# Even and odd value columns as the two halves, and an earlier order of loads, in a fused attention and MLP kernel

## The chip, the cores and the metric

The kernel runs on one core of one Trainium2 chip. The time is the device time of one execution in microseconds (us). For each kernel I quote the median of the fast runs and their range. A run more than 1.5% above the fastest of its kernel counts as slow and is left out. The kernel before took 374.89 us (three runs, 374.56 to 375.86).

The engines are named as the profile names them: PE is the matmul engine (TensorE), PEld its weight loads, DVE the vector engine, ACT the scalar engine, POOL the GpSimd engine, SP the sync engine. A "q" behind a name (SPq, POOLq) means that the engine issued a DMA.

## The reference, cut to what matters

Causal attention with a decay, over 8 batches, 8 heads, 576 tokens and 64 columns a head; then a dense two-layer MLP on the 4608 tokens, whose 512 input channels are the 8 heads side by side.

```python
cum = np.cumsum(np.log(np.clip(f, 0.0001, 1.0)), axis=-1)
scores = q @ k.T / 8 + cum[:, :, :, None] - cum[:, :, None, :]      # causal
attn = softmax(scores)
x = (attn @ v).transpose(0, 2, 1, 3).reshape(B * S, H * D)         # channel = 64 * head + column
h = x @ w_in                                                       # 512 -> 2048
out = (h / (1 + np.exp(-h))) @ w_out                               # 2048 -> 512
```

Everything is fp32 outside; the kernel works in bf16. The decay on the key's side is one weight per key, so the kernel multiplies the value rows by it.

## The kernel before

The work on TensorE is one long list. The first 128 tokens of each batch ("first blocks") are done first, since they give the MLP something to do: `turn0` transposes q and k, `scores0` makes scores and exponentials, `convert_v0` turns the fp32 value rows into weighted bf16 ones on GpSimd, `out0` multiplies and divides, `back0` transposes the result into the MLP's input. The remaining tokens follow in a main loop (`scores`, `attend`, `divide`). MLP chunks fill TensorE's gaps: `fill(us)` takes steps until that many microseconds are spent.

```python
def load_v0(b):
    t = stage.tile([P, H, D], FP32, ...)
    nc.sync.dma_start(out=t[:, :, :], in_=v[b, :, 0:P, :].rearrange("h p d -> p h d"))

# one chunk cc = (g, e) of 128 channels: half e (columns 32e to 32e+31) of the four heads j of group g
w_in_v = moe_w_in.rearrange("(g j e r) f -> g e j r f", g=NCC // 2, j=4, e=2)
def load_w_in(c0, c1):
    for cc in range(NCC):                                     # NCC = 4 chunks
        nc.gpsimd.dma_start(out=w_in_bf[:, cc, c0:c1], in_=w_in_v[cc // 2, cc % 2, :, :, c0:c1])

def after(ap):                    # the sync queue waits here until that piece of a weight has landed
    nc.sync.dma_start(out=junk[0:1, 0:16], in_=ap)

def convert_v(b, c):                                          # 32 of them; convert_v0, 8, is alike
    nc.gpsimd.tensor_tensor(
        out=vp[r, c, :, :],
        in0=vst[b][c][r, :, :],
        in1=w_bf[r, c + 1, b * H : (b + 1) * H, None].to_broadcast([n, H, D]),
        op=ALU.mult,
    )
# ... cut ...
def step():                       # one MLP chunk: up-projection m1 (x -> h), or down-projection m2 (h -> out)
    if can1 and can2:
        can1 = f1 <= f2 or g1 > g2 + 1        # alternate, by the share done of each
    ...

weights_scan()
turn0(0); turn0(1); weights(); scores0(0); convert_v0(0)
turn0(2); convert_v0(1); load_w_in(0, W1)                     # W1 = half of the 2048 columns
out0(0); scores0(1); turn0(3); convert_v0(2); back0(0)
out0(1); scores0(2); convert_v0(3); back0(1)
out0(2); scores0(3); back0(2); out0(3); back0(3)
ready.add(0)
# ... cut: the second half of w_in in two quarters, with q and k of batches 4 and 5 between ...
fill(7.0)
convert_v0(4); convert_v0(5)
for i in range(WQ): load_w_out(i)
after(w_out_bf[0:1, NFC - 1, DM - 16 : DM])
# ... cut: loads of the main loop's first q, k and of batch 0's value rows ...
two_more(4, 0.9)                                              # first blocks of batches 4 and 5
while at["m1"] < NFC: step()
ready.add(1)
while at["m1"] < 2 * NFC: step()
open2["w"] = True
fill(8.0)
convert_v0(6); convert_v0(7)
two_more(6, 0.9)
cast_qk(0); cast_qk(1); transposes(0); transposes(1)
for c in range(NM): convert_v(0, c)
while at["m2"] < M2_OF[0]: step()
ready.add(2)
# ... cut: the main loop ...
```

The softmax here doesn't subtract the row's maximum and nothing guards it: scores larger than these inputs give would overflow.

## Time and profile before

| Reading (kernel before) | us |
|---|---|
| median time; span of the profiled execution | 374.9; 373.9 |
| PE busy | 343.8 (92%) |
| first MLP matmul; MLP matmuls without a stall from | 26.3; 28.5 |
| first half of w_in landed; all of w_out landed | 28.5; 58.4 |
| first transposes for the main loop issued; first main scores | 75.2; 79.7 |
| one value conversion on GpSimd | 1.08 to 1.11 |

The whole page first: busy time of each engine with the number of instructions; TensorE's busy share and its granted clock in tenths over 40 equal slices of the span (9.3 us each); the queue of GpSimd's DMAs with packets, megabytes and share; two groups of instructions (what comes out, what goes in, count, total busy us, mean ns, idle before).

```profile
PE 343.8 (92%) x3621; PEld 190.4 (51%) x3621; DVE 206.5 (55%) x334; ACT 237.4 (64%) x416; POOL 148.0 (40%) x248
...
PE   2759999969997998899799999999999999999994
...
PEclk9957999969999999999999999999999999999998
...
q0 software_dynamic: 10752, 6.31, 11.6%
...
L358 POOL TENSOR_TENSOR vp<-vf,w_bf 128x512 bf16<-128x512 f32 (+1 forms) x32 | 34.3, 1079 | 6.8 <-DMA vf<-in_v_dram 6.1
...
L291 POOL TENSOR_TENSOR v<-vf,w_bf 128x512 bf16<-128x512 f32 x8 | 8.9, 1107 | 14.8 <-DMA vf<-in_v_dram 9.6
```

TensorE is the bottleneck, and the digits show where it isn't full: in the first three slices, in the ninth (75 to 84 us), and here and there up to the twentieth. The rest is solid. The clock digits fall in the third and fourth slices and in the ninth.

The waits of TensorE (total us, times, longest) show the two that belong to the MLP: for `gt`, the activation of an up-projection, and for `osb`, an output buffer.

```profile
PE hp L482 <- DVE gt L491: 8.3, 10, 1.4
...
PE hp L482 <- ACT osb L517: 2.8, 1, 2.8
```

By stretches (window; its length; PE, PEld, DVE, ACT and POOL busy with instructions; granted clock; DMA share; GB/s), nearly all of the 8.3 us lies before 212 us, and TensorE is full after it:

```profile
92.00:212.00 120.00, 111.56 (x1333) 59.66 (x1333) 74.91 (x105) 86.74 (x146) 58.52 (x95) 1.00 0.68 147
212.00:340.00 128.00, 128.00 (x1341) 70.24 (x1339) 76.81 (x121) 90.31 (x162) 46.95 (x74) 1.00 0.48 106
```

What the ninth slice waits for is on the sync queue's timeline (start us, length us, what). The line `junk<-w_out_bf` is the wait for w_out; everything behind it stands in a line.

```profile
58.37 0.50 SPq L188 DMA_DIRECT2D junk<-w_out_bf  x1
...
73.54 1.58 SPq L520 DMA_DIRECT2D out_dram<-osb  x3
75.23 2.98 SPq L372 DMA_TRANSPOSE qkT<-qkb  x2
```

TensorE's timeline gives the other ends: one turn of q and k (32 matmuls), the first long run of MLP matmuls, and the first scores of the main loop. The bracket is the idle time before it and what ended it.

```profile
14.79 1.08 PE L251 MATMUL tp<-sel,qkb 128*64 128x64 bf16 x32
...
28.51 9.70 PE L482 MATMUL hp<-x,w_in_bf 128*128 128x512 bf16 x33 [0.23 <-DMA w_in_bf<-in_moe_w_in_dram]
...
79.68 0.61 PE L402 MATMUL sc<-qkT 64*128 64x128 bf16 x8 [0.37 <-DMA qkT<-qkb]
```

So two chains run beside TensorE's work. One goes from the first blocks to the MLP's start. The other goes from w_out through the sync queue to the transposes and the main loop's start.

### The profile page before, as it was taken

To read this page: it belongs to the slowest core of one execution; us is meant where nothing else is said; L and a number is where in the kernel's file an instruction comes from. 1 tells how busy PE (TensorE), PEld (TensorE's weight loads), DVE (VectorE), ACT (ScalarE), POOL (GpSimd) and SP (SyncE) were. 2 spreads that over 40 slices of the span, in tenths; PEclk is the share of its full clock that TensorE was granted. 3 is DMA by queue.
4 is the path that set the end of the run, shared out by engine and by line. 5 is a ranking of instruction groups with operands and counts; after the bars stand their busy time and mean duration, and the time that the engine had idled before them with its cause. 6 is when DMAs were issued, how large, how long until landed. Compare 5 with 4: busy or idle time off the path is not lost.

```text
span 373.9 us, 9022 instructions
## 1 busy us (share of the span) xinstructions
PE 343.8 (92%) x3621; PEld 190.4 (51%) x3621; DVE 206.5 (55%) x334; ACT 237.4 (64%) x416; POOL 148.0 (40%) x248
## 2 busy tenths in 40 slices
PE   2759999969997998899799999999999999999994
PEld 2623575536644444455454555655554555555652
DVE  3644881425557656663754956656756656443430
ACT  4534782448875857767777878679779675445331
POOL 6656711360963740922734464464464301000000
PEclk9957999969999999999999999999999999999998
DMA  8599796899569538756954985984963000100112
GB/s 159 93 135 182 121 205 128 193 244 188 128 158 216 120 97 186 171 93 143 199 125 98 198 132 139 223 171 99 198 134 79 30 30 29 57 30 30 56 57 56
DMA packets 143066, 47.95 MB, mean 128 GB/s; under 512 B 132720, under 2 KB 137840, under 8 KB 143024
## 3 DMA queue, kind: packets, MB, share of 16 engines
q1 hardware_dynamic: 132272, 41.06, 49.9%
q0 software_dynamic: 10752, 6.31, 11.6%
q8 instruction: 28, 0.46, 0.5%
q14 instruction: 14, 0.11, 0.1%
HBM read 36.85 MB, written 9.44 MB: 124 GB/s over the span
## 4 chain that ended last, share of the span: by engine, by line
PE 67%; DMA 14%; DVE 6%; ACT 4%; SPq 3%; issue 3%; POOL 2%; ACTq 0%; POOLq 0%
PE po L508 29%; PE hp L482 23%; PE dn L433 8%; PE sc L402 6%; DMA w_out_bf<-in_moe_w_out_dram 4%; DMA vf<-in_v_dram 4%; DVE rec L456 4%; DMA w_in_bf<-in_moe_w_in_dram 3%; SPq L143 2%; ACT u L409 2%; DMA qkb<-in_q_dram 2%; DVE gt L491 1%; ACT th L490 1%; DMA qkT<-qkb 1%; POOL v L291 1%
## 5 line engine op out<-in xcount | busy, mean ns | idle before, releaser
L482 PE MATMUL hp<-x,w_in_bf 128*128 128x384 bf16 (+2 forms) x832 | 150.8, 320 | 12.5 <-DVE gt L491 8.3
L491 DVE SCALAR_TENSOR_TENSOR gt<-th,hp 128x384 bf16<-128x384 bf16 (+2 forms) x208 | 102.1, 516 | 85.8 <-ACT th L490 84.4
L508 PE MATMUL po<-w_out_bf,gt 128*128 128x512 bf16 x576 | 143.2, 381 | 0.0
L490 ACT ACTIVATE th<-hp 128x384 bf16<-128x384 f32 (+2 forms) x208 | 93.9, 475 | 57.5 <-PE hp L482 54.1
L482 PEld LDWEIGHTS <-w_in_bf 128*128 128x128 bf16 x832 | 78.9, 99 | 73.6 <-issue 21.9
L409 ACT ACTIVATE u<-sc 128x1024 bf16<-128x1024 f32 (+1 forms) x96 | 89.7, 990 | 13.8 <-PE sc L402 13.8
L464 POOL TENSOR_TENSOR x<-nm,rec 128x384 bf16<-128x384 f32 (+1 forms) x48 | 35.2, 761 | 123.5 <-DVE rec L456 114.1
L508 PEld LDWEIGHTS <-gt 128*128 128x128 bf16 x576 | 53.9, 98 | 53.7 <-issue 3.5
L456 DVE RECIPROCAL rec<-rec 128x224 f32<-128x224 f32 x32 | 47.4, 1524 | 18.4 <-ACT rec L448 18.4
L414 DVE TENSOR_TENSOR u<-u,maskf 128x1024 bf16<-128x1024 bf16 x32 | 27.7, 867 | 29.5 <-ACT u L409 29.3
L517 ACT ACTIVATE osb<-po 128x512 f32<-128x512 f32 x36 | 21.7, 603 | 25.3 <-PE po L508 21.0
L358 POOL TENSOR_TENSOR vp<-vf,w_bf 128x512 bf16<-128x512 f32 (+1 forms) x32 | 34.3, 1079 | 6.8 <-DMA vf<-in_v_dram 6.1
L402 PE MATMUL sc<-qkT 64*128 64x128 bf16 (+3 forms) x384 | 22.9, 241 | 0.4 <-DMA qkT<-qkb 0.4
L339 POOL CAST qkb<-qf 128x384 bf16<-128x384 f32 x32 | 17.5, 546 | 9.5 <-DMA qf<-in_q_dram 9.4
L402 PEld LDWEIGHTS <-qkT 64*128 64x128 bf16 x384 | 13.7, 96 | 14.0 <-issue 10.3
L339 POOL CAST qkb<-kf 128x384 bf16<-128x384 f32 x32 | 19.8, 619 | 1.3 <-DMA kf<-in_k_dram 1.3
L433 PE MATMUL dn<-u,vp 128*32 128x128 bf16 (+3 forms) x768 | 20.0, 237 | 0.0
L448 ACT ACTIVATE rec<-dn 128x448 f32<-128x448 f32 x16 | 8.7, 543 | 16.2 <-PE dn L433 16.2
L433 PEld LDWEIGHTS <-vp 128*32 128x32 bf16 x768 | 17.2, 97 | 3.1
L251 PE MATMUL tp<-sel,qkb 128*64 128x64 bf16 x256 | 10.8, 277 | 6.7 <-DMA qkb<-in_q_dram 6.3
L451 ACT ACTIVATE nm<-dn 128x448 f32<-128x448 f32 x32 | 15.6, 545 | 0.0
L291 POOL TENSOR_TENSOR v<-vf,w_bf 128x512 bf16<-128x512 f32 x8 | 8.9, 1107 | 14.8 <-DMA vf<-in_v_dram 9.6
(53 smaller groups left out, 178.0 us busy)
## 6 DMA issues: line engine op xcount, KB each, us to landing
vf<-in_v_dram SPq DMA_DIRECT2D x32, 256.0 KB, 5.3
out_dram<-osb SPq DMA_DIRECT2D x32, 256.0 KB, 2.5
qf<-in_q_dram SPq DMA_DIRECT2D x64, 96.0 KB, 2.9
kf<-in_k_dram SPq DMA_DIRECT2D x64, 96.0 KB, 2.7
w_out_bf<-in_moe_w_out_dram POOLq DMA_DIRECT2D x4, 512.0 KB, 12.9
qkb<-in_q_dram POOLq DMA_DIRECT2D x8, 128.0 KB, 6.9
qkb<-in_k_dram POOLq DMA_DIRECT2D x8, 128.0 KB, 6.6
w_in_bf<-in_moe_w_in_dram POOLq DMA_DIRECT2D x4, 256.0 KB, 10.7
```

The costliest lines, as they stand in the source:

```text
L339: nc.gpsimd.tensor_copy(out=t2[:, c0 : c0 + NR, :].rearrange("p c x -> p (c x)"), in_=t[:, :, :, :].rearrange("p c h d -> p (c h d)"),)
L358: nc.gpsimd.tensor_tensor(out=vp[r, c, :, :], in0=vst[b][c][r, :, :], in1=w_bf[r, c + 1, b * H : (b + 1) * H, None].to_broadcast([n, H, D] ...
L402: nc.tensor.matmul(sc[:, i, o - c0 : o - c0 + q1 - q0], lhsT=kt, rhs=t[r, q0:q1], start=True, stop=True,)
L409: nc.scalar.activation(out=u[:, :, c0:c1], in_=sc[:, :, 0 : c1 - c0], func=ACT.Exp, scale=scale)
L414: nc.vector.tensor_tensor(out=x, in0=x, in1=maskf[:, None, :].to_broadcast([P, 2, SM]), op=ALU.mult)
L433: nc.tensor.matmul(dn[HD * j : HD * (j + 1), q0:q1], lhsT=w, rhs=us[n][:, i, o : o + q1 - q0], start=(kb == 0), stop=(kb == NM),)
L456: nc.vector.reciprocal(out=recs[qd][:, r], in_=recs[qd][:, r])
L464: eng.tensor_tensor(out=xg(g)[:, cc, g0 : g0 + c1 - c0], in0=nm[:, c0:c1], in1=rec[:, c0:c1], op=ALU.mult,)
L482: nc.tensor.matmul(hp[:, :], lhsT=w_in_bf[:, cc, fc * P : (fc + 1) * P], rhs=xg(g)[:, cc, :], start=(cc == 0), stop=(cc == NCC - 1),)
L490: nc.scalar.activation(out=th[:, :], in_=hp[:, :], func=ACT.Tanh, scale=0.5)
L491: nc.vector.scalar_tensor_tensor(out=gt[:, fc, :], in0=th[:, :], scalar=1.0, in1=hp[:, :], op0=ALU.add, op1=ALU.mult,)
L508: nc.tensor.matmul(po[:, :], lhsT=gt[:, fc, tb * P : (tb + 1) * P], rhs=w_out_bf[:, fc, :], start=(fc == 0), stop=(fc == NFC - 1),)
```

## The change

The intent: w_in's rows are matched to channels. Before, one chunk of 128 channels was the first 32 columns of four heads and the next the last 32. If the two chunks are instead the even and the odd columns, then one partition needs two neighbouring rows of w_in, and a quarter loads in two transfers instead of four. For this the value rows must lie as [even columns, odd columns] per head. The conversion does that on the way: it reads the fp32 row as it came and writes its elements alternately into two halves. With the shorter loads, the order is moved: w_in earlier, w_out directly behind it; the first blocks one batch deeper in the pipeline; and three loops that forced MLP steps to a certain point are dropped, so that `fill` spreads them.

The core of the diff, with cuts:

```diff
-    v0 = [const.tile([P, H, D + 1], BF16, name=f"v0_{b}") for b in range(B)]
+    v0 = [const.tile([P, H, 2, HD + 1], BF16, name=f"v0_{b}") for b in range(B)]
...
-    w_in_v = moe_w_in.rearrange("(g j e r) f -> g e j r f", g=NCC // 2, j=4, e=2)
-    def load_w_in(c0, c1):
-        for cc in range(NCC):
-            nc.gpsimd.dma_start(
-                out=w_in_bf[:, cc, c0:c1], in_=w_in_v[cc // 2, cc % 2, :, :, c0:c1]
-            )
+    w_in_v = moe_w_in.rearrange("(g p e) f -> g p e f", g=NCC // 2, e=2)
+    def load_w_in(i):
+        c0, c1 = i * DFF // WQ, (i + 1) * DFF // WQ
+        for g in range(NCC // 2):
+            nc.gpsimd.dma_start(
+                out=w_in_bf[:, 2 * g : 2 * g + 2, c0:c1], in_=w_in_v[g, :, :, c0:c1]
+            )
...
     def convert_v0(b):
         nc.gpsimd.tensor_tensor(
-            out=v0[b][:, :, 0:D],
-            in0=vf0.pop(b)[:, :, :],
-            in1=w.to_broadcast([P, H, D]),
+            out=v0[b][:, :, :, :].rearrange("p h e r -> p h r e"),
+            in0=vf0.pop(b)[:, :, :, :],
+            in1=w_bf[:, 0, b * H : (b + 1) * H, None, None].to_broadcast([P, H, HD + 1, 2]),
             op=ALU.mult,
         )
-        nc.gpsimd.tensor_copy(out=v0[b][:, :, D : D + 1], in_=w)
...
     def convert_v(b, c):
-            out=vp[r, c, :, :],
-            in0=vst[b][c][r, :, :],
-            in1=w_bf[r, c + 1, b * H : (b + 1) * H, None].to_broadcast([n, H, D]),
+            out=vp[r, c, :, :, :].rearrange("p h e r -> p h r e"),
+            in0=vst[b][c][r, :, 0:HD, :],
+            in1=w_bf[r, c + 1, b * H : (b + 1) * H, None, None].to_broadcast([n, H, HD, 2]),
...
     scores0(0)
     convert_v0(0)
+    turn0(1)
+    mask0(0)
+    scores0(1)
+    load_w_in(0)
+    convert_v0(1)
+    out0(0)
     turn0(2)
...
-    fill(7.0)
     convert_v0(4)
+    load_v0(6)
+    load_w_out(2)
     convert_v0(5)
-    for i in range(WQ):
-        load_w_out(i)
+    load_v0(7)
+    load_w_out(3)
...
+    fill(9.0)
+    two_more(4, 0.9)
...
-    while at["m1"] < NFC:
-        step()
     ready.add(1)
-    while at["m1"] < 2 * NFC:
-        step()
...
-    while at["m2"] < M2_OF[0]:
-        step()
     ready.add(2)
```

The new `load_v0` also fills a column of ones beside each half, by a small GpSimd `memset`, so that the division's denominator comes out of the same matmul.

More of the change, by code (lines that the diff above doesn't have):

```diff
@@ L126, in load_v0 @@
     def load_v0(b):
-        t = stage.tile([P, H, D], FP32, name=f"vf{b % 4}", tag=f"vf{b % 4}")
-        nc.sync.dma_start(out=t[:, :, :], in_=v[b, :, 0:P, :].rearrange("h p d -> p h d"))
+        t = stage.tile([P, H, HD + 1, 2], FP32, name=f"vf{b % 4}", tag=f"vf{b % 4}")
+        nc.gpsimd.memset(t[:, :, HD, :], 1.0)
+        nc.sync.dma_start(
+            out=t[:, :, 0:HD, :].rearrange("p h r e -> p h (r e)"),
+            in_=v[b, :, 0:P, :].rearrange("h p d -> p h d"),
+        )
         vf0[b] = t
@@ L161, in load_v @@
             vst[b] = []
-        t = stage.tile([P, H, D], FP32, name=f"vf{c}", tag=f"vf{c}")
+        t = stage.tile([P, H, HD + 1, 2], FP32, name=f"vf{c}", tag=f"vf{c}")
         r = slice(0, P) if c < NR else slice(ST, P)
         nc.sync.dma_start(
-            out=t[r, :, :],
+            out=t[r, :, 0:HD, :].rearrange("p h r e -> p h (r e)"),
             in_=v[b, :, P + c * P : min(S, P + (c + 1) * P), :].rearrange("h p d -> p h d"),
@@ L168, in load_v @@
         vst[b].append(t)
-    w_in_v = moe_w_in.rearrange("(g j e r) f -> g e j r f", g=NCC // 2, j=4, e=2)
-    def load_w_in(c0, c1):
-        for cc in range(NCC):
+    w_in_v = moe_w_in.rearrange("(g p e) f -> g p e f", g=NCC // 2, e=2)
+    WQ = 4
+    def load_w_in(i):
+        c0, c1 = i * DFF // WQ, (i + 1) * DFF // WQ
+        for g in range(NCC // 2):
             nc.gpsimd.dma_start(
-                out=w_in_bf[:, cc, c0:c1], in_=w_in_v[cc // 2, cc % 2, :, :, c0:c1]
+                out=w_in_bf[:, 2 * g : 2 * g + 2, c0:c1], in_=w_in_v[g, :, :, c0:c1]
             )
-    WQ = 4
     def load_w_out(i):
@@ L283, in scores0, with mask0 @@
         )
-        x = u[:, :, :, :].rearrange("p i a t -> p (i a) t")
+    def mask0(b):
+        x = u0[b][:, :, :, :].rearrange("p i a t -> p (i a) t")
         nc.vector.tensor_tensor(
@@ L289, in convert_v0 @@
     def convert_v0(b):
-        w = w_bf[:, 0, b * H : (b + 1) * H, None]
         nc.gpsimd.tensor_tensor(
-            out=v0[b][:, :, 0:D],
-            in0=vf0.pop(b)[:, :, :],
-            in1=w.to_broadcast([P, H, D]),
+            out=v0[b][:, :, :, :].rearrange("p h e r -> p h r e"),
+            in0=vf0.pop(b)[:, :, :, :],
+            in1=w_bf[:, 0, b * H : (b + 1) * H, None, None].to_broadcast([P, H, HD + 1, 2]),
             op=ALU.mult,
         )
-        nc.gpsimd.tensor_copy(out=v0[b][:, :, D : D + 1], in_=w)
     xqs: dict[int, bass.AP] = {}
@@ L305, in out0 @@
             nc.tensor.matmul(
-                dn[:, h // 4, h % 4, 0 : D + 1],
+                dn[:, h // 4, h % 4, 0 : D + 2],
                 lhsT=u[:, h % 2, h // 2, :],
-                rhs=v0[b][:, h, :],
+                rhs=v0[b][:, h, :, :],
                 start=True,
@@ L312, in out0 @@
         rec = recp.tile([P, 2, 4], FP32, name="rec0", tag="rec0")
-        nc.vector.reciprocal(out=rec[:, :, :], in_=dn[:, :, :, D])
+        nc.vector.reciprocal(out=rec[:, :, :], in_=dn[:, :, :, HD])
         xq = xqp.tile([P, 2, 2, 4, HD], BF16, name="xq", tag="xq")
@@ L317, in out0 @@
                 out=xq[:, g, :, :, :].rearrange("p e j r -> p j e r"),
-                in0=dn[:, g, :, 0:D].rearrange("p j (e r) -> p j e r", e=2),
+                in0=dn[:, g, :, 0 : D + 2].rearrange("p j (e r) -> p j e r", e=2)[:, :, :, 0:HD],
                 in1=rec[:, g, :, None, None].to_broadcast([P, 4, 2, HD]),
@@ L350, in convert_v @@
         if c == 0:
-            vbf[b] = vpool.tile([P, NM, H, D], BF16, name="vp", tag="vp")
+            vbf[b] = vpool.tile([P, NM, H, 2, HD], BF16, name="vp", tag="vp")
         vp = vbf[b]
@@ L355, in convert_v @@
             r = slice(ST, P)
-            nc.gpsimd.memset(vp[0:ST, c, :, :], 0.0)
+            nc.gpsimd.memset(vp[0:ST, c, :, :, :], 0.0)
         n = r.stop - r.start
         nc.gpsimd.tensor_tensor(
-            out=vp[r, c, :, :],
-            in0=vst[b][c][r, :, :],
-            in1=w_bf[r, c + 1, b * H : (b + 1) * H, None].to_broadcast([n, H, D]),
+            out=vp[r, c, :, :, :].rearrange("p h e r -> p h r e"),
+            in0=vst[b][c][r, :, 0:HD, :],
+            in1=w_bf[r, c + 1, b * H : (b + 1) * H, None, None].to_broadcast([n, H, HD, 2]),
             op=ALU.mult,
@@ L429, in quad @@
                 elif kb == 0:
-                    w = v0[b][:, h, what * HD : (what + 1) * HD]
+                    w = v0[b][:, h, what, 0:HD]
                 else:
-                    w = vbf[b][:, kb - 1, h, what * HD : (what + 1) * HD]
+                    w = vbf[b][:, kb - 1, h, what, :]
                 nc.tensor.matmul(
@@ L567, in fill @@
         return True
-    W1 = DFF // 2
     weights_scan()
     turn0(0)
-    turn0(1)
     weights()
@@ L579 @@
     convert_v0(0)
-    turn0(2)
-    convert_v0(1)
-    load_w_in(0, W1)
-    out0(0)
-    scores0(1)
+    turn0(1)
[4 more added lines that the diff above has]
+    out0(0)
+    turn0(2)
+    mask0(1)
+    scores0(2)
+    convert_v0(2)
+    out0(1)
+    back0(0)
+    load_w_in(1)
     turn0(3)
-    convert_v0(2)
-    back0(0)
-    out0(1)
-    scores0(2)
+    mask0(2)
+    scores0(3)
     convert_v0(3)
+    out0(2)
     back0(1)
-    out0(2)
-    scores0(3)
+    mask0(3)
+    out0(3)
     back0(2)
-    out0(3)
     back0(3)
     ready.add(0)
-    load_w_in(W1, W1 + W1 // 2)
+    load_w_in(2)
+    load_w_in(3)
+    after(w_in_bf[0:1, NCC - 1, DFF // 2 - 16 : DFF // 2])
     load_qk0(4)
+    load_v0(4)
     load_qk0(5)
-    load_w_in(W1 + W1 // 2, DFF)
+    load_v0(5)
+    load_w_out(0)
+    load_w_out(1)
     nc.gpsimd.memset(maskf[:, P + 2 * P : SM], 1.0)
@@ L606 @@
         nc.gpsimd.tensor_copy(out=maskf[:, c * P : (c + 1) * P], in_=maskf[:, 0:P])
-    after(w_in_bf[0:1, NCC - 1, W1 - 16 : W1])
-    load_v0(4)
-    load_v0(5)
-    after(w_in_bf[0:1, NCC - 1, DFF - 16 : DFF])
-    load_v0(6)
-    load_v0(7)
+    after(w_out_bf[0:1, 2 * NFC // WQ - 1, DM - 16 : DM])
     def two_more(b, piece):
@@ L617, in two_more @@
         scores0(b)
+        mask0(b)
         fill(piece)
         scores0(b + 1)
+        mask0(b + 1)
         fill(2 * piece)
@@ L627, in two_more @@
         back0(b + 1)
-    fill(7.0)
     convert_v0(4)
+    load_v0(6)
+    load_w_out(2)
     convert_v0(5)
-    for i in range(WQ):
-        load_w_out(i)
+    load_v0(7)
+    load_w_out(3)
+    load_qk0(6)
+    load_qk0(7)
+    fill(9.0)
+    two_more(4, 0.9)
     after(w_out_bf[0:1, NFC - 1, DM - 16 : DM])
@@ L638 @@
             load_tails(0)
-    for c in range(NM):
-        load_v(0, c)
-    two_more(4, 0.9)
-    load_qk0(6)
-    load_qk0(7)
-    while at["m1"] < NFC:
-        step()
     ready.add(1)
-    while at["m1"] < 2 * NFC:
-        step()
     open2["w"] = True
@@ L652 @@
     convert_v0(7)
+    for c in range(NM):
+        load_v(0, c)
     two_more(6, 0.9)
```

## The prediction

> **What bounds the kernel.** TensorE: the page gives it 92% of a 373.9 us span (343.8 busy), and in the windows view it is 100% busy from 240 to 340 us. So the time is TensorE's work plus its idle and half-clock time, most of it before 212 us:
> 1. Start. Timeline: the four first blocks' out matmuls start at 14.1, 17.1, 20.5, 23.5; the first MLP matmuls start at 26.3, stall on w_in, and run steadily from 28.5. The granted clock is 0.50 from 20 to 33 us. The Trainium skill ("TensorE: Matmul & The Clock Gate", Part 1) says the clock halves after an idle window of about 3.4 us and returns after one of sustained work; the trace agrees (back about 5 us after 28.5).
> 2. 75 to 84 us. Chain of waits: w_out lands (58.4), the sync queue issues for 15 us (0.5 each), transposes issue at 75.2 and land at 79.6. Output stores queue behind those loads, so TensorE waits 2.8 us for an output buffer, then has clock 0.50 until 84.5.
> 3. 92 to 212 us: 8.4 us idle, nearly all "hp <- gt" waits (8.3 us), where up to eight up-projection chunks run without a down-projection between. After 212 the two alternate and TensorE never waits.
>
> **What the change does.**
> - First blocks one batch deeper. By the order on TensorE and VectorE the first out matmuls start about 1.5 us sooner, and the last block has no turn in its way: MLP input ready at 24 instead of 26.3.
> - First w_in quarter issued at about 10.5 us instead of 15, 8 issues of 0.67 us instead of 12, half the bytes before the first chunk; landed by about 20. MLP steady from 24 instead of 28.5: 3.6 us net of the matmuls already done there. Fewer gaps may keep the clock up: 1 us.
> - w_out is issued straight after w_in; DMA nearly idles at 14 to 16 and 38 to 42 us now. w_out lands at 48 instead of 58.4; transposes at 63. Stall and half clock of point 2 mostly go: 5 us.
> - The forced loops are gone, so about 5 us more MLP work is kept as filler. By the step rule, up- and down-projection then alternate through the loop: 5 to 6 of the 8.4 us.
> - Against it: filler runs out at the end of blocks 4 and 5 (2 us). The value conversion (1.04 us, 40 times) now writes with a stride of 33 elements; "GPSIMD Engine Reference", section 7, warns of reads with steps over 8 bytes, not of writes. I expect 1.1 to 1.6 us each; GpSimd is 40% busy, so little counts. Four memsets delay its start by 0.5 us.
>
> Sum: -3.6 -1 -5 -5.5 +2, about -13; I keep 12 for new waits on w_in or w_out.
>
> **Predicted:** 363 us, 8 in 10 within 355 to 370. Faster by over 2%: 0.76; within 2%: 0.21; slower by over 2%: 0.03.
>
> **What would show it.** Steady MLP matmuls from 23 to 25 us; w_out landed by 50; first main scores near 66 instead of 79.7; no wait for an output buffer near 75; "hp <- gt" waits under 3 us; the tail from 340 still full, only earlier.
>
> **What would make it wrong.** w_in quarters or w_out later than TensorE wants them (DMA moved only 34 to 138 GB/s from 16 to 24 us while GpSimd computed); conversions of 2 us or more, slowing VectorE through the shared port; transposes still late on the sync queue; the clock falling again in the new bubble.

## The result, and the profile after

The changed kernel took 370.6 us (fast runs 369.8, 370.2 and 371.1, one slow run at 375.7 left out), against 374.7 beside it. The ratio is 0.988 (95% interval 0.984 to 0.992), so by the 2% measure it is the same. I forecast 363 and a range up to 370: it gained 4 us where I expected 12. A ratio here is the mean time of one kernel's fast runs over the mean of the other's fast runs of the same rounds, so it isn't quite the ratio of the medians that I quote.

| us | before | after | forecast |
|---|---|---|---|
| MLP matmuls without a stall from | 28.5 | 28.3 | 24 |
| first half of w_in landed | 28.5 | 23.5 | 20 for a quarter |
| w_out landed | 58.4 | 53.1 | 48 |
| first transposes issued | 75.2 | 69.2 | 63 |
| first main scores | 79.7 | 73.5 | 66 |
| one value conversion | 1.08 to 1.11 | 2.6 | 1.1 to 1.6 |

(`junk<-w_in_bf` on the sync queue, behind its wait, gives the landing of w_in.) The page after, the same lines:

```profile
PE 339.4 (92%) x3577; PEld 191.5 (52%) x3621; DVE 210.9 (57%) x334; ACT 238.2 (65%) x416; POOL 194.9 (53%) x244
...
PE   3669979898899999999999999999999999999994
...
PEclk9999989999999999999999999999999999999999
...
q0 software_dynamic: 6592, 6.29, 11.4%
...
L362 POOL TENSOR_TENSOR vp<-vf,w_bf 128x512 bf16<-128x512 f32 (+1 forms) x32 | 79.4, 2594 | 6.2 <-DMA vf<-in_v_dram 5.6
...
L296 POOL TENSOR_TENSOR v<-vf,w_bf 128x528 bf16<-128x528 f32 x8 | 20.0, 2603 | 12.4 <-DMA vf<-in_v_dram 10.2
```

GpSimd is busy 47 us longer, and these two lines account for it: their sum went from 43.2 to 99.4 us (its spans overlap the next instruction a little, so the sum grew by more than the engine's busy time). The packets on its DMA queue fell from 10,752 to 6592 (experiment 5 looks at what these packets are). 44 matmul records are missing from this trace (the weight loads are all there), so PE's busy time reads a little low.

TensorE's waits: the activation waits have shrunk from 8.3 to 1.5 us and the wait for an output buffer is gone. The wait of the main loop's scores for their transposes has grown from 0.4 to 4.2 us.

```profile
PE sc L406 <- DMA qkT<-qkb: 4.2, 3, 1.6
...
PE hp L486 <- DVE gt L495: 1.5, 4, 0.9
```

By stretches, the gain in the middle came as forecast, 5.2 us more busy in the same window, with GpSimd at 86 us instead of 59:

```profile
92.00:212.00 120.00, 116.77 (x1435) 64.36 (x1445) 80.41 (x113) 92.13 (x160) 86.36 (x100) 1.00 0.84 163
```

The sync queue and TensorE show the two chains. Both ends of the w_out chain moved up by 5 to 6 us, not by 12:

```profile
53.11 0.51 SPq L192 DMA_DIRECT2D junk<-w_out_bf  x1
...
69.16 2.98 SPq L376 DMA_TRANSPOSE qkT<-qkb  x2
79.70 1.27 SPq L376 DMA_TRANSPOSE qkT<-qkb  x1
```

```profile
13.27 1.92 PE L255 MATMUL tp<-sel,qkb 128*64 128x64 bf16 x32
...
28.30 10.16 PE L486 MATMUL hp<-x,w_in_bf 128*128 128x512 bf16 x42 [0.22 <-issue]
...
73.51 0.40 PE L406 MATMUL sc<-qkT 64*128 64x128 bf16 x8 [1.11 <-DMA qkT<-qkb]
```

The turn, which took 1.08 us in the line shown of before, takes 1.92 here. The MLP starts no sooner. And GpSimd's timeline shows what w_out stood behind:

```profile
38.47 2.56 POOL L296 TENSOR_TENSOR v<-vf,w_bf 128x528 bf16<-128x528 f32 x1 [7.84 <-DMA vf<-in_v_dram]
...
40.68 0.81 POOL L186 DMA_DIRECT2D w_out_bf<-in_moe_w_out_dram  x1
...
68.24 7.08 POOL L362 TENSOR_TENSOR vp<-vf,w_bf 128x512 bf16<-128x512 f32 x3 [5.56 <-DMA vf<-in_v_dram]
75.82 2.51 POOL L362 TENSOR_TENSOR vp<-vf,w_bf 64x512 bf16<-64x512 f32 x1
78.39 0.59 POOL L343 CAST qkb<-qf 128x384 bf16<-128x384 f32 x1
```

The last two quarters of w_out are issued by GpSimd in order, at 40.7 and 44.7, each behind a conversion. The first two are late as well: they go at 26.3 and 28.4, behind four slow conversions, where the repaired kernel of experiment 2 issues them at 23.2 and 24.7. Four more conversions block the casts for the third pair of heads from 68.2 until 78.4, and so the third transpose (79.70 above). The vector engine is touched too. Two masks of the same shape, one with GpSimd issuing DMAs beside it and one with a conversion beside it, take very different times:

```profile
11.98 0.68 DVE L291 TENSOR_TENSOR u<-u,maskf 128x1024 bf16<-128x1024 bf16 x1
15.84 2.21 DVE L291 TENSOR_TENSOR u<-u,maskf 128x1024 bf16<-128x1024 bf16 x1
```

That agrees with the Trainium skill ("GPSIMD Engine Reference", section 1, Specifications), which says that GpSimd shares its SBUF interfaces with VectorE and that they contend when the VectorE instruction has two SBUF inputs, as the mask has; that section gives no size. One pair of lines isn't an experiment, but the repair below shortens the conversions, and the longest of the first four masks there is 1.15 us.

### The profile page after: what moved, and what is told of

Read it like the earlier page. It is cut to its first block, busy times and chain, and to the rows that moved or that the text cites. A ratio compares the mean times of both kernels' runs of the same rounds, so it can differ in the third digit from the quotient of the medians.

```text
span 368.4 us, 8980 instructions
## 1 busy us (share of the span) xinstructions
PE 339.4 (92%) x3577; PEld 191.5 (52%) x3621; DVE 210.9 (57%) x334; ACT 238.2 (65%) x416; POOL 194.9 (53%) x244
## 3 DMA queue, kind: packets, MB, share of 16 engines
q0 software_dynamic: 6592, 6.29, 11.4%
## 4 chain that ended last, share of the span: by engine, by line
PE 67%; DMA 13%; POOL 5%; SPq 5%; issue 4%; DVE 3%; ACT 2%; POOLq 0%; ACTq 0%
PE po L512 27%; PE hp L486 26%; PE dn L437 7%; PE sc L406 6%; DMA vf<-in_v_dram 6%; SPq L147 4%; DMA qkT<-qkb 2%; POOL vp L362 2%; DMA w_out_bf<-in_moe_w_out_dram 2%; POOL v L296 2%; DMA w_in_bf<-in_moe_w_in_dram 1%; DMA qkb<-in_k_dram 1%; ACT u L413 1%; DVE u L418 1%; DVE rec L460 1%
## 5 line engine op out<-in xcount | busy, mean ns | idle before, releaser
L495 DVE SCALAR_TENSOR_TENSOR gt<-th,hp 128x384 bf16<-128x384 bf16 (+2 forms) x208 | 103.2, 515 | 83.1 <-ACT th L494 81.1
L512 PE MATMUL po<-w_out_bf,gt 128*128 128x512 bf16 x534 | 141.4, 382 | 3.0 <-issue 1.0
L494 ACT ACTIVATE th<-hp 128x384 bf16<-128x384 f32 (+2 forms) x208 | 95.9, 473 | 64.5 <-PE hp L486 63.2
L362 POOL TENSOR_TENSOR vp<-vf,w_bf 128x512 bf16<-128x512 f32 (+1 forms) x32 | 79.4, 2594 | 6.2 <-DMA vf<-in_v_dram 5.6
L468 POOL TENSOR_TENSOR x<-nm,rec 128x384 bf16<-128x384 f32 (+1 forms) x48 | 36.6, 789 | 75.3 <-DVE rec L460 57.4
L418 DVE TENSOR_TENSOR u<-u,maskf 128x1024 bf16<-128x1024 bf16 x32 | 33.5, 1046 | 27.3 <-ACT u L413 27.3
L296 POOL TENSOR_TENSOR v<-vf,w_bf 128x528 bf16<-128x528 f32 x8 | 20.0, 2603 | 12.4 <-DMA vf<-in_v_dram 10.2
L255 PE MATMUL tp<-sel,qkb 128*64 128x64 bf16 x256 | 12.2, 296 | 6.7 <-DMA qkb<-in_q_dram 5.2
L343 POOL CAST qkb<-kf 128x384 bf16<-128x384 f32 x32 | 17.2, 536 | 1.1 <-DMA kf<-in_k_dram 1.1
```

Of the source, the lines that this page charges most:

```text
L343: nc.gpsimd.tensor_copy(out=t2[:, c0 : c0 + NR, :].rearrange("p c x -> p (c x)"), in_=t[:, :, :, :].rearrange("p c h d -> p (c h d)"),)
L362: nc.gpsimd.tensor_tensor(out=vp[r, c, :, :, :].rearrange("p h e r -> p h r e"), in0=vst[b][c][r, :, 0:HD, :], in1=w_bf[r, c + 1, b * H : ...
L418: nc.vector.tensor_tensor(out=x, in0=x, in1=maskf[:, None, :].to_broadcast([P, 2, SM]), op=ALU.mult)
L468: eng.tensor_tensor(out=xg(g)[:, cc, g0 : g0 + c1 - c0], in0=nm[:, c0:c1], in1=rec[:, c0:c1], op=ALU.mult,)
L494: nc.scalar.activation(out=th[:, :], in_=hp[:, :], func=ACT.Tanh, scale=0.5)
L495: nc.vector.scalar_tensor_tensor(out=gt[:, fc, :], in0=th[:, :], scalar=1.0, in1=hp[:, :], op0=ALU.add, op1=ALU.mult,)
```

## The experiments

My theory after the result: the order and the loads are worth about what I forecast, and the slow conversion gives most of it back, by delaying w_out and the casts. Rivals: (a) the loads are bound by something else, so a fast conversion brings little; (b) the forecast gains of the order were never there. A second question came up on the way: what the row pairs of w_in are good for, since the number of transfers was small from the start.

All kernels below give the reference's result, except one that is marked. Each has its own runs of the kernel before, whose medians lay between 374.2 and 375.3 us.

### 1. What the conversion costs by itself: micro

The changed kernel, with seven forms of the multiply on 512 elements a partition added to GpSimd after its last work, each three times. Source and destination have the same sizes; only the order of reading and writing differs.

```diff
+    for _ in range(3):
+        # 1: row to row                     2: as the change: write pairs alternately into two halves, 64 bytes apart
+        # 3: read every second fp32, write in a row     4: write pairs every 16 bytes
+        # 5: write single elements 8 bytes apart        6: runs of 32, row to row
+        # 7: write single elements 64 bytes apart
+        nc.gpsimd.tensor_tensor(...)
```

> The change with 21 extra GpSimd multiplies of 512 elements behind its last work (seven forms of address, three times each; results unused). In order: 1 row to row, 2 the change's form (pairs written 64 bytes apart), 3 read every second fp32 and write in a row, 4 pairs written as neighbours, 16 bytes from pair to pair, 5 single elements written 8 bytes apart, 6 row to row in runs of 32, 7 single elements written 64 bytes apart in runs of 16. Known: 1 near 1.04 us, 2 near 2.5 us. If short runs of two are what costs: 4 near 2.5, 7 and 5 near 1.04 to 1.2. If distant writes are what costs: 7 near 2.5, 4 near 1.04. 3 near 1.04 if a read step of 8 bytes is free[...], near 1.5 if not.

GpSimd's timeline, one round in that order (forms 5 and 6, left out, took 1.35 and 1.04 us):

```profile
297.85 1.04 POOL L733 TENSOR_TENSOR md<-ms,w_bf 128x512 bf16<-128x512 f32 x1
298.85 2.51 POOL L739 TENSOR_TENSOR md<-ms,w_bf 128x512 bf16<-128x512 f32 x1
300.94 1.16 POOL L745 TENSOR_TENSOR md<-ms,w_bf 128x512 bf16<-128x512 f32 x1
302.18 1.04 POOL L751 TENSOR_TENSOR md<-ms,w_bf 128x512 bf16<-128x512 f32 x1
...
305.72 2.45 POOL L769 TENSOR_TENSOR md<-ms,w_bf 128x512 bf16<-128x512 f32 x1
```

The repeats agree within 0.02 us. The Trainium skill ("Perfetto Trace Analysis", "GPSIMD Engine Instruction") advises to time this engine from start to start and not by the span. So read, form 1 holds it for 1.00 us, form 2 for 2.09, form 3 for 1.24 and form 7 for 2.53 (up to the next round's start at 308.25). The ranking of slow and fast is the same, though the span of form 2 overstates it by 0.4 us. Short runs aren't the cost (form 4 writes pairs as form 2 does, and has the same span as row to row, 1.04 us; 1.12 against 1.00 from start to start); neither is a read of every second fp32 (form 3). What costs is a write that lands 64 bytes from the last one, alone (form 7) or by turns (form 2).

The Trainium skill ("GPSIMD Engine Reference", section 7, the table of pitfalls) warns of reads with a step of more than 8 bytes and says nothing of writes. Form 3 has a read step of exactly 8 bytes and pays 0.12 us by its span (0.24 from start to start); that agrees. The cost of distant writes is what that section lacks. The kernel's one run took 369.65 us; its added work stands beside a TensorE that is busy longer, and I draw nothing from the time.

### 2. The same layout written in rows: read_stride

The output is written in its own order, and the fp32 input is read with a step of two.

```diff
         nc.gpsimd.tensor_tensor(
-            out=v0[b][:, :, :, :].rearrange("p h e r -> p h r e"),
-            in0=vf0.pop(b)[:, :, :, :],
-            in1=w_bf[:, 0, b * H : (b + 1) * H, None, None].to_broadcast([P, H, HD + 1, 2]),
+            out=v0[b][:, :, :, :],
+            in0=vf0.pop(b)[:, :, :, :].rearrange("p h r e -> p h e r"),
+            in1=w_bf[:, 0, b * H : (b + 1) * H, None, None].to_broadcast([P, H, 2, HD + 1]),
```

(and `convert_v` in the same way)

> The change with one thing altered: the value conversion on GpSimd writes 32 or 33 neighbouring elements in a row and reads every second fp32 instead (it read in a row and wrote pairs 66 or 64 bytes apart). Theory A (the slow conversion, 2.6 us where it was 1.04, holds up casts, transposes and the w_out issue behind it on GpSimd): conversions back to 1.0 to 1.2 us, the wait of the main scores for transposes (4.2 us) under 1 us, 362 to 366 us. Rival B (the loads in the new order get in each other's way: value rows of blocks 4 and 5 take 17 us to land beside w_out): 369 to 371 us, as the change, and w_out still lands near 53 us.

It took 362.7 us (362.1 to 363.4), ratio 0.968 (0.964 to 0.972): faster than both kernels, and 7.9 us less than the change, by medians (by the ratios, 2.0% of 374.9, it is 7.5). From its page, its sync queue and TensorE:

```profile
L362 POOL TENSOR_TENSOR vp<-vf,w_bf 128x512 bf16<-128x512 f32 (+1 forms) x32 | 35.4, 1114 | 6.1 <-DMA vf<-in_v_dram 5.4
```

```profile
47.59 0.50 SPq L192 DMA_DIRECT2D junk<-w_out_bf  x1
...
63.52 3.02 SPq L376 DMA_TRANSPOSE qkT<-qkb  x2
```

```profile
68.90 0.40 PE L406 MATMUL sc<-qkT 64*128 64x128 bf16 x8
```

w_out lands 5.5 us sooner than in the change, at the 48 that I forecast; the first transposes go at 63.5 (forecast 63). The main loop starts 4.6 us sooner, and its scores never wait for a transpose, where the change lost 3.1 us after its first main scores (4.2 less the 1.1 in front of them). These two make 7.7 us, which is about the difference in time. This is the theory's result, and rival (a) is out: the conversion was the whole shortfall in size.

How it costs them is less simple than the theory has it. Of the 4.6 us only 1.1 was a wait for transposes. TensorE's own list was 3.4 us late before that: the turn of blocks 6 and 7 starts at 59.74 in the change and at 56.31 here. Of this, 0.9 us is the MLP's later start. Another 0.9 comes by the end of the bubble in TensorE's list behind blocks 4 and 5, where a mask beside a slow conversion took 1.70 us against 0.69. The last 1.7 comes in the MLP work behind that bubble, which in the change begins at about half speed. The same four matmuls, in the change and in read_stride:

```profile
52.25 1.91 PE L512 MATMUL po<-w_out_bf,gt 128*128 128x512 bf16 x4
```

```profile
49.72 1.03 PE L512 MATMUL po<-w_out_bf,gt 128*128 128x512 bf16 x4
```

So "the clock falling again in the new bubble", which the prediction had named, did happen in the change. Its transposes were later still (issued 5.6 us later than here), so they came last. These two runs don't say what each chain is worth alone. order_only (experiment 4) helps: its list is on time (56.19), its transposes are nearly as late (68.15), and it waits 3.8 us for them and starts the main loop at 72.6. So late transposes alone are worth about 3.7 us.

The repair does not show that each forecast step held, and the MLP's start did not: 27.5 us without a stall, not 24.

### 3. Which of the conversions: read_v0 and read_v

Only the 8 conversions of first blocks repaired, or only the 32 of the main loop, each by the edit above.

> Only the 8 conversions of first-block values read with a stride and write in a row (near 1.1 us); the 32 others stay at 2.6 us. Theory A1 (what costs is that w_out sits behind those conversions on GpSimd): as with all repaired, near 363 us, w_out landed near 47.6. Theory A2 (what costs is that the casts for the transposes sit behind the four conversions near 68 us): w_out near 47.6 and first main scores near 69, but waits of the scores for transposes stay near 4 us and DVE masks stay slow: 365 to 367 us.

> Only the 32 conversions of the main loop are repaired; the 8 first ones stay at 2.6 us. A1: w_out still lands near 53, first main scores near 73.5, no later waits: 367 to 369 us. A2: 363 to 365 us.

read_v0 took 366.8 us (366.0 to 367.6; ratio 0.980, 0.975 to 0.984), about half of the repair. Its w_out lands at 48.4 and its first transposes go at 64.3, as in the full repair, but the next ones only at 75.4, since their casts stand behind the four slow conversions of batch 0. So about half of the cost lies with the first conversions. That the rest lies with the four conversions of batch 0 follows from the difference and from these late transposes; the run that should show it directly is the next one, and it doesn't.

read_v took 372.7 us, but its runs spread from 369.7 to 374.1 (ratio 0.994, 0.988 to 1.001), where most kernels here keep within 2 us. It met neither forecast (367 to 369, or 363 to 365). The profile fell on its slowest run. In it one mask that began just before two slow conversions took 7.39 us (its like took 2.21 in the change), TensorE waited 6.7 us for it, and the MLP started at 32.5. So the slow first conversions also cost through VectorE, and here by more than through the queue. It fits that w_out is still late (51.2 landed, transposes 75.5), but I call the run inconclusive: with one profile I can't say whether that mask is what made this kernel's runs differ, nor why it isn't faster than the change.

### 4. One part of the change at a time: order_only, layout_only, layout_read

order_only has the change's order, but the old value layout, conversion and w_in rows (16 transfers of quarter chunks). layout_only has the old order with the change's layout, slow conversion and row pairs. layout_read is layout_only with the repaired conversion.

```diff
 # order_only, against the change
-    w_in_v = moe_w_in.rearrange("(g p e) f -> g p e f", g=NCC // 2, e=2)
+    w_in_v = moe_w_in.rearrange("(g j e r) f -> g e j r f", g=NCC // 2, j=4, e=2)
     def load_w_in(i):
-        for g in range(NCC // 2): ...
+        for cc in range(NCC): ...
 # layout_only and layout_read, against before
+    the value tiles, the conversion and load_w_in of the change (of read_stride), in the order of before
```

> The change's order of loads and deeper pipeline, with the value layout and conversion of before and w_in in four transfers a quarter. Theory A: 362 to 367 us. Rival B: 369 to 372 us, since the order of the loads is the same as in the change.

> The order of before, with the change's value layout, conversion and row pairs of w_in (two transfers each time). Theory A: slower than before by 3 to 9 us (378 to 384 us), with the conversions at 2.6 us. Rival B: within 1 us of before, for GpSimd was only 40% busy.

> The order of before with the new value layout, row pairs and the repaired conversion. If layout and order add up: 375.0 - (368.4 - 362.7) = 369 us. If the layout's faster w_in only pays where w_out is issued straight behind it: 372 to 374 us.

| median us (ratio to before) | old layout | new layout, slow conversion | new layout, repaired |
|---|---|---|---|
| old order | 374.9 (1) | 372.9 (0.996) | 371.3 (0.990) |
| new order | 368.4 (0.984) | 370.6 (0.988) | 362.7 (0.968) |

The order alone is worth 1.6%, the layout with the repaired conversion alone 1.0%, both 3.2%: roughly the sum and a bit more (layout_read's runs spread from 368.5 to 373.3, so its 1.0% is the least sure of the three). Rival (b) is out as well, though order_only fell between its two forecasts. The slow conversion costs 0.6% in the old order (the two intervals overlap) and 2.0% in the new. My theory had forecast 378 to 384 us for layout_only, so there it missed; I read it so that the same GpSimd time hurts where the order has put w_out and the casts right behind it. And the new layout with the slow conversion is no better than the old layout, in the new order.

In layout_read w_out lands at 52.0, but the sync queue then stands 8.2 us at three output stores and the first transposes still go at 75.0. The old forced loops stand in between, which is probably why. So the earlier landing does not reach the main loop in the old order.

order_only left a question. Its conversions are fast and its order is that of read_stride, and still w_out lands at 51.8 instead of 47.6. The differences that touch the loads are w_in's rows and the number of its transfers.

### 5. What the row pairs are good for: four_transfers and split_rows

four_transfers is read_stride with twice the number of w_in transfers, one for even and one for odd rows. split_rows is four_transfers with w_in's rows by the old rule. **Its result is wrong on purpose** (relative error 1.39: w_in's rows no longer match the channels); the work is the same.

```diff
 # four_transfers, against read_stride
-            nc.gpsimd.dma_start(
-                out=w_in_bf[:, 2 * g : 2 * g + 2, c0:c1], in_=w_in_v[g, :, :, c0:c1]
-            )
+            for e in range(2):
+                nc.gpsimd.dma_start(
+                    out=w_in_bf[:, 2 * g + e, c0:c1], in_=w_in_v[g, :, e, c0:c1]
+                )
 # split_rows, against four_transfers
-    w_in_v = moe_w_in.rearrange("(g p e) f -> g p e f", g=NCC // 2, e=2)
+    w_in_v = moe_w_in.rearrange("(g j e r) f -> g e j r f", g=NCC // 2, j=4, e=2)
-                    out=w_in_bf[:, 2 * g + e, c0:c1], in_=w_in_v[g, :, e, c0:c1]
+                    out=w_in_bf[:, 2 * g + e, c0:c1], in_=w_in_v[g, e, :, :, c0:c1]
```

> All conversions repaired, and each w_in quarter loaded in four transfers (each half of a pair by itself) instead of two: same layout, same bytes, 16 issues instead of 8. If the 5.6 us between the repaired kernel and the one with the order alone come from the number of transfers on the GpSimd queue: w_out(1) issued near 32 instead of 24.7, w_out landed near 52 instead of 47.6, first main scores near 72.6 after a wait of 3 to 4 us for a transpose, 367 to 369 us. If they come from the layout of the values: 362 to 364 us.

> All conversions repaired, new value layout, w_in in four transfers a quarter, but with the old rule which row of w_in goes to which partition (blocks of 32 rows, two strides instead of one). The result is wrong on purpose: rows and columns no longer match. [...]If this split is what the kernel with the order alone lost: w_out lands near 52 us, first main scores near 72.5, 367 to 369 us. If the value layout was it: w_out near 49, 362 to 364 us.

four_transfers took 362.6 us (361.7 to 364.2; ratio 0.969), the same as read_stride. split_rows took 367.6 (365.2 to 367.9; ratio 0.978, 0.974 to 0.983), about 5 us more, and is order_only's time within the noise. The packets of all DMA by size and those of GpSimd's queue (from the page), and the landing of w_out (from the sync queue's timeline); four_transfers first, then split_rows:

```profile
DMA packets 139034, 47.93 MB, mean 133 GB/s; under 512 B 128176, under 2 KB 134320, under 8 KB 138992
...
q0 software_dynamic: 6720, 6.29, 11.4%
```

```profile
49.05 0.51 SPq L193 DMA_DIRECT2D junk<-w_out_bf  x1
```

```profile
DMA packets 145178, 47.95 MB, mean 131 GB/s; under 512 B 134320, under 2 KB 140464, under 8 KB 145136
...
q0 software_dynamic: 12864, 6.32, 12.1%
```

```profile
52.45 0.50 SPq L193 DMA_DIRECT2D junk<-w_out_bf  x1
```

In split_rows the first main scores come at 73.3 us, after a wait of 4.8 us for their transposes.

So the number of transfers is worth nothing here in time, and the row rule is worth 5 us. That is what the two runs show. The packets don't explain it as simply as I first thought. The same 16 transfers take 6144 packets more under the old rule, which is 3 for each of their 2048 rows (16 times 128). But a row is not cut into four: between 512 bytes and 2 KB both kernels have 6144 packets (134,320 less 128,176, and 140,464 less 134,320), so all the added ones are under 512 bytes, and the queue's megabytes grow by only 0.03. The records in the packed traces give the sizes on this queue: 6144 packets of 1024 bytes in both, and beside them 576 packets of 4 bytes in four_transfers and 6720 in split_rows. So the old rule moves the same rows whole and adds three packets of 4 bytes for each. (The expectation for split_rows had taken them for pieces of rows.)

What differs is how the row index runs: in one step under the new rule, and in two (four heads of 32 rows) under the old. Under the old rule the queue's packets took about 3 us more of each DMA engine (12.1% of 366.1 us against 11.4% of 361.0), an issue took GpSimd 0.67 us instead of 0.57, and a w_in transfer landed 6.8 us after its issue instead of 4.4 (medians), so w_out's first quarter was issued at 29.3 instead of 26.0. What the small packets are for, and whether they are what costs the time, stays open. From 17 to 24 us, order_only moved 114 GB/s, split_rows 123 and four_transfers 143.

### 6. The deeper order of the first blocks: shallow

read_stride with the first four blocks in TensorE's old order; GpSimd's order stays the change's.

```diff
     turn0(0)
+    turn0(1)
     weights()
     scores0(0)
-    convert_v0(0)
-    turn0(1)
     mask0(0)
-    scores0(1)
+    convert_v0(0)
+    turn0(2)
     load_w_in(0)
     convert_v0(1)
     out0(0)
-    turn0(2)
+    scores0(1)
+    turn0(3)
     ...
```

> All conversions repaired, everything of the change except the deeper pipeline of the first four blocks: their order on TensorE, VectorE and ScalarE is that of before, GpSimd's order that of the change. In the change MLP starts at 26.5 to 27.5 us against 26.3 before, so the deeper order may have gained nothing: then 362 to 364 us. If it hides 2 us that the half clock ate: 365 to 366 us.

It took 365.8 us (364.0 to 366.4; ratio 0.974), 3 us more than read_stride. So the deeper order is worth about 3 us, but not by the way I had in mind: the MLP's first matmul comes at 25.7, earlier than read_stride's 26.6. What is later is the loads, and TensorE's list. The weights come behind the second turn, so the first conversion starts at 12.2 instead of 9.0, w_in is issued at 13.2 instead of 10.0, and w_out lands at 51.9 instead of 47.6. TensorE reaches the turn of blocks 6 and 7 at 58.6 instead of 56.3, with its MLP matmuls at half speed for longer at the start and again behind the bubble, and then waits 1.5 us for the transposes. The main loop's first scores are at 72.7, 3.8 us later.

### 7. The forced steps and the bubble: forced and fill7

```diff
 # forced, against read_stride
+    while at["m1"] < NFC: step()
     ready.add(1)
+    while at["m1"] < 2 * NFC: step()
     ...
+    while at["m2"] < M2_OF[0]: step()
     ready.add(2)
 # fill7, against read_stride
-    fill(9.0)
+    fill(7.0)
```

> All conversions repaired, but the two forced stretches of MLP work of before are put back (all up-projection of groups 0 and 1 before the down-projection opens, all of group 0's down-projection before the main loop). The prediction gave 5 to 6 us to their removal. If so: waits of up-projection matmuls for VectorE back near 8 us in the main loop, 367 to 369 us. If not: 362 to 364 us.

> All conversions repaired, and 7 instead of 9 us of up-projection ahead of blocks 4 and 5, so that the filler lasts through them. If the 2 us bubble at 46 to 48 us is on the critical path: 1 to 2 us faster than with 9 (361 to 362 us). If the value rows of block 5 (converted by 40.1 us) then come late, or the end is set by the loads behind w_out: no gain, 362.5 to 364 us.

forced took 370.2 us (369.4 to 370.6; ratio 0.986), 7.5 us more than read_stride, where I had forecast 5 to 6 for this part. The wait for activations is back:

```profile
PE hp L486 <- DVE gt L495: 6.5, 9, 1.4
```

(0.7 us in read_stride.) The first transposes are also back at 74.6. So the alternation of up- and down-projection is worth what its waits show; that the rest is the sync queue's is not shown.

fill7 took 363.4 us (362.2 to 364.7), not different from read_stride. It asks whether the bubble at the end of blocks 4 and 5, which I had charged with 2 us, can be moved to advantage. It is there: TensorE idles about 2 us from 46.5 to 49.7 us in the change. In fill7 it is gone, and the turn of blocks 6 and 7 starts at 53.2 instead of 56.3. But TensorE then waits 2.6 us for the transposes, and the main scores come at 68.3 against 68.9. So the gain on TensorE's list is given back at the other chain.

### 8. The late start of the MLP: warm, early_tr, warm_early

In the change and in read_stride a turn takes 1.92 us where it can take 1.08. warm adds matmuls without use (128x512, on a constant tile) to read_stride, nine before the first turn and twelve more in the gaps that follow.

```diff
+    wz = const.tile([P, 512], BF16, name="wz")
+    def warm(n): ...                      # n matmuls into a free PSUM tile
+    warm(9)
     turn0(0)
+    warm(1)
     ...
```

> All conversions repaired, plus 21 dummy matmuls of 512 columns on a constant tile: nine before the first input lands and one to three in each gap of the first four blocks. In the change the turns of blocks 1 to 3 take 1.92 us where a full clock gives 1.08, though the recorded clock says 1.00. If the half clock is why the MLP starts at 26.6 to 27.5 and not at 24: turns near 1.1 us, MLP from 23 to 24.5 us, and 359 to 361 us. If VectorE's and ScalarE's steps set that chain: MLP at 26 or later, 362 to 364 us.

warm took 363.7 us (363.1 to 366.8; ratio 0.970), no faster than read_stride, where I had forecast 359 to 361 if the half clock was the cause. Its profile is that of its slowest run, 366.8. But its start did what it should:

```profile
16.22 1.08 PE L263 MATMUL tp<-sel,qkb 128*64 128x64 bf16 x32
...
23.29 9.66 PE L494 MATMUL hp<-x,w_in_bf 128*128 128x512 bf16 x43 [0.46 <-ACT x L342]
...
72.16 0.40 PE L414 MATMUL sc<-qkT 64*128 64x128 bf16 x8 [4.06 <-DMA qkT<-qkb]
```

The turns run at 1.08 us and the MLP starts at 23.3, a little before my 24, and much later TensorE waits 4.1 us for the transposes. So the late start was the half clock, and w_in would have been there. The 3 to 4 us won at the start are lost again in two places. By the turn of blocks 6 and 7 (55.45 against 56.31) 0.9 us of them is left: TensorE waited 2.1 us for the value rows of block 5 and then ran at half speed until about 49 us. And w_out lands at 49.9 here, 2.3 us later than in read_stride, so the transposes are late too.

The granted clock in the records is of no use for this. It gives 1.00 from 12 to 16 us in the change (and its page's digits are 9 throughout the start), with the turns at close to half their speed. The Trainium skill ("TensorE: Matmul & The Clock Gate", Part 1, "Seeing it yourself") warns that clock events in traces have been unreliable. This trace agrees, and durations of a known shape are the better clock.

early_tr moves the first two pairs' casts and transposes ahead of batch 0's value loads and of blocks 6 and 7, with one more buffer for them; warm_early is both edits.

```diff
-    qktp = ctx.enter_context(tc.tile_pool(name="qktp", bufs=3))
+    qktp = ctx.enter_context(tc.tile_pool(name="qktp", bufs=4))
...
     convert_v0(7)
+    cast_qk(0)
+    cast_qk(1)
+    transposes(0)
+    transposes(1)
     for c in range(NM):
         load_v(0, c)
     two_more(6, 0.9)
-    cast_qk(0)
-    cast_qk(1)
-    transposes(0)
-    transposes(1)
```

> All conversions repaired; the first two transposes are issued on the sync queue before the four value loads of batch 0 instead of behind them and behind two stores (one more buffer for their tile). In the repaired kernel TensorE reaches the main scores at 68.9 us without a wait, so this alone should gain nothing: transposes issued near 59 to 60 us instead of 63.5, 362 to 363.5 us.

> The 21 dummy matmuls and the early transposes together. If the queue of loads behind w_out took the gain of the dummies back: no wait of 4 us before the main scores, which start at 66 to 68 us instead of 72.2, and 359 to 361 us. If the dummies cost as much as they gain by themselves: 362 to 364 us.

early_tr took 364.8 us (363.9 to 365.2; ratio 0.973), 2 us more than read_stride: its transposes go at 60.8 and nothing waits for them, yet the main scores come at 72.0. That is not the work of the edit: by the turn of blocks 6 and 7 TensorE's list is already 3.1 us late (59.4 against 56.3), 1.4 of it by 39 us, before any moved line has run. The MLP matmuls from 27.45 on take 11.66 us for what takes 10.22 in read_stride, and those behind the bubble begin at half speed again. So a kernel's time here can move by 2 to 3 us with when TensorE gets its full speed back; why it came later here isn't known. warm_early took 362.7 (362.1 to 363.8; ratio 0.967), the same as read_stride. There the main scores start at 64.2, nearly 5 us sooner, and then wait for the transposes of the next pairs:

```profile
PE sc L414 <- DMA qkT<-qkb: 6.2, 3, 2.9
```

The next pairs' casts stand behind the conversions of batch 0's values, and those behind the loads of the values. So the gain of an early start is given back, one station further on. A version below 362.6 us I did not find.

## Why the prediction was wrong, point by point

- **"MLP steady from 24 instead of 28.5": wrong in the change (28.3), and the gain of this step was zero.** I took turn durations at full speed, 1.08 us; they took 1.92, and one mask beside a conversion took 2.21 us. warm shows that full-speed turns bring 23.3. In warm they brought no time, since w_out, the value rows and the transposes came no sooner. The deeper order is worth 3 us (shallow), in part through earlier loads.
- **"landed by about 20": the first half of w_in landed at 23.5, and 21.7 after the repair.** TensorE did not wait for w_in in either, so this did no harm.
- **"w_out lands at 48 instead of 58.4; transposes at 63": right only with the repaired conversion** (47.6 and 63.5). In the change they came at 53.1 and 69.2. The output-buffer wait went away as forecast, and the clock digit of the ninth slice is whole again. In its place came the half speed behind the new bubble (1.7 us), which the prediction had among the things that could make it wrong.
- **"5 to 6 of the 8.4 us" for the alternation: right.** The waits went from 8.3 to 1.5 us, and forced lost 7.5 us.
- **"filler runs out at the end of blocks 4 and 5 (2 us)": the bubble exists,** about 2 us of it, but taking it away (fill7) brought no time that the runs could show.
- **The step that failed: "I expect 1.1 to 1.6 us each; GpSimd is 40% busy, so little counts."** The conversion took 2.6 us. And the second half of the sentence is the worse one. GpSimd at 40% on average still stands ahead of w_out and of the third pair's casts, in order, and a slow conversion beside a mask also holds VectorE up. The main loop started 4.6 us later for it and then lost 3.1 us in waits for transposes. The repair of this one point brought 7.9 us, with everything else unchanged. I had it in my list of what would make the prediction wrong ("conversions of 2 us or more"), with the vector engine as the victim, and gave it no share in the sum. Both were hit, the vector engine and the queue behind the conversion. Late transposes alone are worth about 3.7 us (order_only); how the 7.9 us divide between the two isn't shown. I had noted that the skill's warning is for reads, and took that as weak evidence that writes are cheap. It was no evidence.
- **The row pairs: a benefit that I did not see.** I counted issues (8 of 0.67 us instead of 12). Their number is worth nothing (four_transfers); what counts is the order of the rows in a transfer, 5 us (split_rows). Why it does stays open; the added packets of 4 bytes are a trace of it.

That the repaired kernel lands on 363 is partly luck. The start of the MLP, 3.5 us short of my forecast, was, as I reckon it, made up for by what the row pairs and the alternation brought above it.

Open stays read_v's spread, and how far TensorE's list and the chain w_out, sync queue, transposes, conversions must both be moved at once to get below 362 us. fill7 and warm_early only show that a gain on TensorE's list alone is given back at the transposes. Open is also when TensorE returns to full speed behind the bubble, which differs between kernels with the same order.

## What to carry to other kernels

When a layout must be permuted by a GpSimd instruction, let the read take the small stride and the write run in rows, and measure the one instruction before the kernel (2.51 us against 1.16 here): the layout was worth 1.0% alone and another 1.6% on top of the new order, and its wrong direction hid it all. An engine's average busy share says nothing about what stands behind it in its queue: look up which DMA issues and casts follow the instruction that gets longer. For a weight load, try a row order in which the row index runs in one stride, and not only fewer transfers: here the first was worth 5 us and the second nothing. And before packets are read as pieces of the data, look at their sizes.

## What the Trainium skill lacked or had wrong

- "GPSIMD Engine Reference", section 7: among this engine's pitfalls it warns of strided reads and has nothing on writes. Writes 64 bytes apart, single or alternating in pairs, took 2.45 and 2.51 us for 512 elements a partition, against 1.04 in a row; single elements 8 bytes apart took 1.35.
